# Attention scores of all 24 units in plain float32, two heads in row halves

## The chip, the cores and the metric

The kernel runs on one core of a Trainium2 chip. The metric is the device time of one launch in microseconds (us); lower is better. A core has a matrix engine (PE, with its weight loads shown apart as PEld), a vector engine (DVE), a scalar engine (ACT), GpSimd (POOL) and a queue engine that issues the transfers (SP). Each works through its own instructions in order, and the engines wait for one another through semaphores.

## What is computed

The reference is a gated linear attention (an mLSTM cell) over 4 batches, 8 heads, 768 steps and head size 40, and behind it two dense networks over the 3072 tokens:

```
C = f_stab * C + i_stab * (v k^T);  n = f_stab * n + i_stab * k
y_t = sigmoid(o_t) * (C q_t) / max(|n . q_t|, 1)
x = y as 3072 x 320
x = relu(x @ w_in)^2 @ w_out            (320 -> 2048 -> 320)
x = elu(x @ w2_in) @ w2_out             (320 -> 2048 -> 320)
```

The gates enter through running maxima, so that every exponent stays bounded. All inputs are float32.

## The kernel before, in words

**Tiles and stages.** The sequence is cut into 6 chunks of 128 steps. A unit u is one batch of one chunk (24 units, u = 4 x chunk + batch), and a half n = 2u + e holds the four heads of one parity of that unit. In a unit the chunk is done in parallel: scores K Q^T per head (128 x 128), times a matrix of decays, times V, plus what the state C of the chunks before gives. The first network then takes four units as one tile of 512 tokens. Its 6 tiles times 16 blocks of 128 hidden columns are steps k = 0 to 95; each has 8 matmuls into a bank `h` (mm1, line 501) and 8 into three banks `acc` (mm2, line 546), all 512 columns wide. The second network (lines 582, 612, 626) follows as steps 96 to 191. Weights and activations are held as a rounded high part and a low part (`w`, `xh`/`xl`, `ghi`/`glo`), so that products of fp32r operands reach float32 accuracy.

**How attention and network share the engines.** Attention of tile j + 1 is woven into the steps of tile j. Every step takes one turn t of the attention, four turns to a unit (k = t mod 4). The order in which instructions are issued is the order of the program on every engine. Up to step 19 it is written out by hand: the string ORDER (line 45) is a list of words, each a letter (a task, table at line 788) and a number. So `S16` is the scores of half 16, `p16` the product with its decays, `t7` the transposes of unit 7, `n7` its division, `h7` and `l7` the split of the transposed result, `V8` the values of unit 8 and `Z8` their evacuation, `118`, `216` and `316` are mm1 of step 18 and the two halves of mm2 of step 16, `A` and `F` are the activations and the low part of a step, and `M`, `E` the mask and the exponentials of a half. Behind ORDER the turns do the same by rule, in `attn_pre`, `attn_pe`, `attn_mul`, `attn_post` and `attn_last` (lines 421 to 477).

**The scores.** There are two ways. Halves n < 16 (units 0 to 7, NPLAIN, line 35) use `pair_scores` (line 303). Queries and keys lie as plain float32 in one tile, heads of parity 0 in rows 0 to 39 and heads of parity 1 in rows 64 to 103. Eight matmuls with 40 rows alternate between the halves of the array and write two PSUM banks, `s` and `in` (units 0 to 3 use a bank of `acc` in place of `in`). The profile shows each plain float32 matmul as two records. Halves from 16 up (units 8 to 23) use stacked parts: the host repeats queries and keys three times (120 rows, 480 KB per half); `qk_hi` (line 267, ACT) rounds all to fp32r, `qk_stack` (line 272, DVE, two instructions) turns one third of the rows into the low part, with the factors in `qkm`; then each head is one fp32r matmul over 120 rows (line 320), four to a half, into bank `s` alone. For these units queries are loaded a second time in the row-half layout, as `qp` (line 233), because `values` needs them so.

**The bank `in`.** It is one PSUM bank with several users, each of which waits until the readers of the one before are done: the second half of the plain scores (read by `emit_P`, DVE), the product of queries and state in `values` (line 331, read by `evac`, DVE line 360), the transposes of the normalized result (line 389, read by `x_hi`, ACT line 399, and `x_lo`, DVE lines 406 and 407), and the gates of chunk 1.

**Turns of a unit before.** k = 0: exponentials of the first half, `norm` of unit u - 1, scores and product of the first half. k = 1: exponentials of the second half, `o_tanh`, `wk_mult`, transposes of unit u - 1, scores and product of the second half, `x_hi`, `x_lo`. k = 2: `qk_hi`, `mask` and `qk_stack` for unit u + 1, and then `values` and `evac`. k = 3: loads for unit u + 2.

Of the kernel before, what the change touches and what calls it, by code (L numbers as in the profile page):

```python
# [6 lines left out]
F32 = mybir.dt.float32  # L7
# [14 lines left out]
L = 128  # L22
# [9 lines left out]
KVO = 2 * DM + H * VW  # L32
TT = 4 * L
NTILE = NT // TT
NPLAIN = 16
N0 = 2 * B
TEND = 4 * (NU - 1) + 7
NK = 20
# [9 lines left out]
n1 s3 L0 i2 v5 R3 e6 p6 b2 c2 a2 C1 U1 i3 t1 B8 o2 z4 i2 v6 e7 r0 Q9 p7 M9 k3 z5 n2 v7 o3 E9 h1 z6 z7 b3 l1 n3  # L48
i4 t2 h2 c3 l2 i3 t3 h3 i1 S8 M8 E8 Q10 R4 R5 B11 B10 b4 l3 10 o4 L1 11 a3 A0 p9 H2 L2 R6 12 H3 F0 c4 c5 A1 L3
c6 20 30 M11 21 G2 G3 a4 k4 p8 V4 Q12 13 H4 L4 F1 b5 b6 M10 E10 31 B12 A2 22 a5 H5 K5 Z4 n4 k5 14 L5 t4 R7 c7  # L50
F2 32 b7 a6 H6 R8 g2 R9 Q11 R10 A3 F3 B13 A4 L6 a7 Q16 F4 B14 h4 l4 c8 b8 R11 a8 c9 b9 o5 15 23 A5 H7 L7 a9
c10 Q14 33 F5 K6 24 H8 L8 Q15 16 S10 p10 17 x2 34 E11 25 D2 Q13 H9 L9 p11 A6 b10 A7 a10 F6 35 26 M12 M13 V5
H10 C2 18 36 27 R12 L10 19 R13 E13 y16 o6 F7 37 Z5 c11 b11 a11 B16 n5 c12 U2 A8 110 b12 F8 H11 b13 L11 a12 c13
t5 h5 l5 B15 E12 k6 A9 M14 B17 28 38 K7 k7 H12 Y16 a13 S12 p13 M15 p12 H13 R14 R15 b14 c14 M16 L12 111 F9 A10
F10 29 M17 V6 Z6 n6 B18 E14 112 39 210 310 t6 L13 A11 211 113 a14 H14 c15 b15 a15 H15 h6 l6 F11 E15 A12 S14
p14 q8 A13 K8 p15 F12 311 o7 E17 212 E16 V7 L14 114 F13 Q17 Q18 B19 L15 115 Z7 n7 g3 312 A14 F14 k8 213 M18 q9
t7 h7 l7 S16 p16 y17 y18 313 Y17 Q19 214 Y18 Q20 116 314 A15 117 A16 F16 E18 S17 y19 215 p17 V8 F15 Y19 S18
p18 B20 315 B21 P15 K9 M21 A17 118 216 119 M20 Z8 o8 n8 E20 A18 F17 k9 t8 h8 D3 M19 E19 316 217 K10 F18 S19
q10 A19 317 120 121 p19 x3 l8 F19 y20 Y20 C3 U3 V9 Z9 Q21 y21 Y21 o9 218 A20 318 219 S20 n9 K11 B22 319 p20
Q22 A21 F21 Q23 B23 F20 q11  # L60
"""


def body(tc, qk, qp, kvo, gates, wq, ident_in, qkm_in, out):
    nc = tc.nc
    pe, act, dve, pool_, sp = nc.tensor, nc.scalar, nc.vector, nc.gpsimd, nc.sync
    es = ExitStack()
# [33 lines left out]
    qkm = constp.tile([3 * D, 2], F32, name="qkm")  # L101
    one = constp.tile([64, 1], F32, name="one")
    dve.memset(msk[0:64], 0.0)
    dve.memset(msk[64:128], -1.0)
# [114 lines left out]
            aw_t.pop(c)  # L219


    kvo_t, qp_t, qk_t, mb_t, raw_t, qS, kS, num_t, S_t, PV_t, xt_t, XT_t, X = ({} for _ in range(13))

    def kvo_load(u):

# [7 lines left out]
    def qp_load(u):
        t = a2.tile([128, 4 * L], F32, tag="qp", name="qp")
        sp.dma_start(out=t, in_=qp[u])
        qp_t[u] = t

    def mb_tile(n):
        if n < NPLAIN and n % 2:
# [16 lines left out]

    def qk_load(n):
        u, e = divmod(n, 2)
        if n >= NPLAIN:
            t = raw_t[n] = a2.tile([3 * D, 2, 4 * L], F32, tag="rqk", name="rqk")  # L260
            sp.dma_start(out=t, in_=qk[n])
            return
        if u not in qk_t:
            qk_t[u] = plain[u % B] if u >= B else wp.tile([128, 2 * WC], F32, tag="w", name="rqk")[:, 0:8 * L].rearrange("p (two t) -> p two t", two=2)
        sp.dma_start(out=qk_t[u][64 * e:64 * e + 48], in_=qk[n, 0:48])

    def qk_hi(n):
        st = a2.tile([3 * D, 2, 4 * L], F32R, tag="qks", name="qks")
        act.activation(out=st, in_=raw_t[n], func=AF.Copy)
        qS[n], kS[n] = st[:, 0], st[:, 1]  # L270

    def qk_stack(n):
        t = raw_t.pop(n)
        for i, st in enumerate((qS[n], kS[n])):
            dve.scalar_tensor_tensor(out=st, in0=st.bitcast(F32), scalar=qkm[:, i:i + 1], in1=t[:, i], op0=ALU.mult, op1=ALU.add)

    def keyed(u):
        return u // B < NCH - 1
# [30 lines left out]
                k1, q1 = (t[64 * e:64 * e + D, x, i * L:(i + 1) * L] for x in (1, 0))  # L309
                pe.matmul(S_t[2 * u + e][:, i, :], lhsT=k1, rhs=q1, start=True, stop=True)  # L310

    def scores(n):
        s = bank(n, "s")
        if n < NPLAIN:
            return [lambda: pair_scores(n // 2, (s, bank(n, "in")))]
        s = s.rearrange("p (h t) -> p h t", h=4)
        k_, q_ = kS.pop(n), qS[n]
        S_t[n] = s
        return [
            lambda i=i: pe.matmul(s[:, i, :], lhsT=k_[:, i * L:(i + 1) * L], rhs=q_[:, i * L:(i + 1) * L], start=True, stop=True)  # L320
            for i in range(4)
        ]
# [15 lines left out]
    def values(u):  # L338
        b = u % B
        t = kvo_t[u]  # L340
        q = qk_t.pop(u)[:, 0] if u in qk_t else qp_t.pop(u)
# [441 lines left out]
    def turned(u):  # L783
# [14 lines left out]
    for word in ORDER.split():
# [116 lines left out]
def _layout(inputs):  # L915
# [12 lines left out]
    qp = np.zeros((NU, 128, 4, L), np.float32)  # L928
    for e in range(2):
        qp[:, 64 * e:64 * e + D] = units_t(inputs["q"]).reshape(NU, D, 4, 2, L)[:, :, :, e]  # L930
    qk = np.concatenate([qk] * 3, axis=1)
    qkm = np.zeros((3 * D, 2), np.float32)
    qkm[2 * D:, 0] = -1.0
    qkm[D:2 * D, 1] = -1.0
# [7 lines left out]
    for pre in ("moe_", "moe2_"):  # L942
# [39 lines left out]
```

## Time and profile before

| what | value |
|---|---|
| median of 3 runs | 800.41 us (798.16 to 804.31) |
| the profiled execution | 797.7 us, of which its span is 795.9 us |
| granted TensorE clock | 0.999 of full speed |
| moved by DMA | 88.22 MB |
| query and key loads of units 8 to 23 | 32 of 480 KB, and 16 of 256 KB (`qp`) |
| query and key loads of units 0 to 7 | 16 of 192 KB |

The page of the profile gives busy time by engine, the span in 40 slices, and the groups of instructions that cost most. The busy time of PE says less than it seems to, because the end of a matmul is modelled and matmuls overlap; starts are what the trace has, and the distance from start to start is the cost. In a timeline each row is a run of alike instructions on one engine: start, length, engine, line, operation, output <- inputs, shape and count, and in brackets how long the engine sat idle before and what ended that. A few records of matmuls are missing from the trace, so a count can be lower than the program's.

### The profile page before, as it was taken

How to read it: one execution, taken by the hardware profiler on the slowest of the kernel's cores; microseconds unless marked ns; L12 is line 12 of the kernel's file. 1: busy time of each engine (PE TensorE's matmuls, PEld its weight loads, DVE VectorE, ACT ScalarE, POOL GpSimd, SP SyncE). 2: the span in 40 equal slices, each digit the busy share in tenths (PEclk: the TensorE clock that was granted, in tenths of full speed). 3: DMA queues.
4: the chain of work that ended last, by engine and by line, in shares of the span. 5: the costliest groups of instructions: out<-in, count | busy, mean ns of one | idle time of the engine just before them, and what ended most of it. 6: DMA issues, size and time to landing. Idle time of an engine off the chain costs nothing.

```text
span 795.9 us, 17791 instructions
## 1 busy us (share of the span) xinstructions
PE 786.7 (99%) x7054; PEld 671.7 (84%) x7058; DVE 548.9 (69%) x946; ACT 529.0 (66%) x1028; POOL 143.5 (18%) x209
## 2 busy tenths in 40 slices
PE   8999999999999999999999999999999999999998
PEld 5688788888888888888888889999999999999997
DVE  5898987667666566555348569867677677677765
ACT  5899868677666776777489667565465565555543
POOL 3224201100000001000012123221222122222221
PEclk9999999999999999999999999999999999999999
DMA  8998434955354656551335710300400401300100
GB/s 238 325 284 247 125 101 149 286 152 155 115 162 129 174 132 177 138 164 37 81 112 182 189 41 2 82 34 2 95 20 1 114 2 26 88 2 2 35 1 34
DMA packets 33257, 88.22 MB, mean 111 GB/s; under 512 B 3735, under 2 KB 7319, under 8 KB 33175
## 3 DMA queue, kind: packets, MB, share of 16 engines
q1 hardware_dynamic: 32887, 86.77, 38.7%
q8 instruction: 55, 0.90, 0.5%
q10 hardware_dynamic: 288, 0.33, 0.1%
q14 instruction: 27, 0.22, 0.1%
HBM read 78.35 MB, written 8.73 MB: 109 GB/s over the span
## 4 chain that ended last, share of the span: by engine, by line
PE 87%; DVE 5%; DMA 4%; issue 1%; POOL 1%; SPq 1%; ACT 0%; POOLq 0%; DVEq 0%; ACTq 0%
PE h L582 21%; PE acc L612 20%; PE acc L546 20%; PE h L501 19%; PE pv L331 2%; DMA mb<-negm_dr 2%; PE in L331 2%; PE s L320 2%; DMA raw<-wq 1%; DMA kvo<-kvo 1%; DVE w L150 1%; DVE ct L140 1%; PE in L389 1%; POOL w L144 1%; DVE glo L530 1%
## 5 line engine op out<-in xcount | busy, mean ns | idle before, releaser
L530 DVE TENSOR_TENSOR glo<-r,ghi 128x512 fp32r<-128x512 f32 x192 | 135.6, 707 | 119.2 <-ACT r L516 94.4
L501 PE MATMUL h<-xh,w 128*128 128x512 f32 x576 | 179.8, 394 | 0.0
L612 PE MATMUL acc<-w,ghi 64*128 64x320 f32 x1472 | 142.3, 306 | 0.0
L520 ACT ACTIVATE r<-h 128x512 f32<-128x512 f32 x96 | 56.6, 589 | 116.8 <-PE h L582 116.8
L523 DVE SCALAR_TENSOR_TENSOR ex<-ex,th 128x512 f32<-128x512 f32 x96 | 83.2, 867 | 66.0 <-ACT ex L522 66.0
L501 PEld LDWEIGHTS h<-xh,w 128*128 128x128 f32 x576 | 108.1, 188 | 23.8
L546 PE MATMUL acc<-ghi,w 128*128 128x512 f32 x480 | 127.7, 395 | 0.0
L612 PEld LDWEIGHTS acc<-w,ghi 64*128 64x128 f32 x1472 | 119.4, 184 | 4.1
L525 POOL TENSOR_SCALAR ghi<-r 128x512 fp32r<-128x512 f32 x96 | 74.2, 773 | 264.4 <-DVE r L524 243.7
L546 PEld LDWEIGHTS acc<-ghi,w 128*128 128x128 f32 x480 | 87.5, 188 | 17.5 <-issue 0.4
L612 PE MATMUL acc<-w,glo 64*128 64x320 f32 x736 | 91.4, 306 | 0.0
L515 ACT ACTIVATE ghi<-r 128x512 fp32r<-128x512 f32 x96 | 60.6, 631 | 43.7 <-PE acc L546 42.4
L582 PE MATMUL h<-x,w 64*128 64x512 f32 x720 | 86.7, 388 | 0.0
L514 ACT ACTIVATE r<-h 128x512 f32<-128x512 f32 x96 | 56.6, 589 | 42.5 <-PE h L501 41.2
L546 PE MATMUL acc<-glo,w 128*128 128x512 f32 x288 | 81.8, 392 | 0.0
L582 PEld LDWEIGHTS h<-x,w 64*128 64x128 f32 x720 | 66.4, 184 | 13.5 <-issue 0.7
L501 PE MATMUL h<-xl,w 128*128 128x512 f32 x192 | 74.9, 390 | 0.0
L524 DVE SCALAR_TENSOR_TENSOR r<-h,ex 128x512 f32<-128x512 f32 x96 | 66.4, 692 | 3.3
L612 PEld LDWEIGHTS acc<-w,glo 64*128 64x128 f32 x736 | 63.4, 184 | 0.0
L546 PEld LDWEIGHTS acc<-glo,w 128*128 128x128 f32 x288 | 53.6, 188 | 11.3
L521 ACT ACTIVATE th<-r 128x512 f32<-128x512 f32 x96 | 60.7, 633 | 3.1
L516 ACT ACTIVATE r<-r 128x512 f32<-128x512 f32 x96 | 60.7, 632 | 2.9
(124 smaller groups left out, 1079.3 us busy)
## 6 DMA issues: line engine op xcount, KB each, us to landing
raw<-wq SPq DMA_DIRECT2D x32, 704.0 KB, 6.7
rqk<-qk SPq DMA_DIRECT2D x32, 480.0 KB, 7.9
kvo<-kvo SPq DMA_DIRECT2D x24, 488.0 KB, 5.3
mb<-negm_dr SPq DMA_DIRECT2D x40, 256.0 KB, 5.4
yr<-y_dr SPq DMA_DIRECT2D x12, 768.0 KB, 8.4
y_dr<-y SPq DMA_DIRECT2D x18, 256.0 KB, 3.7
qp<-qp SPq DMA_DIRECT2D x16, 256.0 KB, 6.2
rqk<-qk SPq DMA_DIRECT2D x16, 192.0 KB, 8.8
```

The source lines that it names most:

```text
L501: lambda i=i, a=a, b_=b_: pe.matmul(h[:, 0:n], lhsT=a, rhs=b_, start=(i == 0), stop=(i == len(seq) - 1))
L514: act.activation(out=r, in_=h, func=AF.Relu)
L515: act.activation(out=hi, in_=r, func=AF.Square)
L516: act.activation(out=r, in_=r, func=AF.Square)
L521: act.activation(out=th, in_=r, func=AF.Tanh, scale=0.5)
L523: dve.scalar_tensor_tensor(out=ex, in0=ex, scalar=1.0, in1=th, op0=ALU.add, op1=ALU.mult)
L524: dve.scalar_tensor_tensor(out=r, in0=h, scalar=0.0, in1=ex, op0=ALU.max, op1=ALU.subtract)
L525: pool_.tensor_scalar(out=hi, in0=r, scalar1=1.0, scalar2=1.0, op0=ALU.mult, op1=ALU.mult)
L530: dve.tensor_tensor(out=lo, in0=r, in1=hi.bitcast(F32), op=ALU.subtract)
L546: ops.append(lambda: pe.matmul(o, lhsT=l_, rhs=r_, start=first and st, stop=last and sp_))
L582: pe.matmul(h[i], lhsT=a[r], rhs=b_[r], start=n == 0, stop=n == len(ops) - 1)
L612: pe.matmul(ACC[l, j][i][:, 0:DM], lhsT=a, rhs=b_, start=m == 0 and not again and n == 0, stop=n == 5 and (not again or m + 2 == NF), skip ...
```

## The change

All units use `pair_scores`. `qk_hi`, `qk_stack`, `qp_load`, the tile `qkm` and its load are gone, as are their words in ORDER (`r`, `y`, `Y`, `q`); queries and keys are loaded once, 192 KB per half. The four tiles `plain` serve the units in turn. In the turns the scores of both halves stand at k = 0 and so do both products; the exponentials of the first half move to turn k = 3 of the unit before, those of the second half to k = 0. In ORDER the words `S17` and `S19` go (the scores of a unit are one word now), `p17`, `p19` and `p21` move up behind the first product of their unit, and `Z8`, `M19`, `E19` and `S18` change places. NPLAIN lives on as NEARLY, for the choice of a tile in `mb_tile`.

```diff
 def qk_load(n):
     u, e = divmod(n, 2)
-    if n >= NPLAIN:
-        t = raw_t[n] = a2.tile([3 * D, 2, 4 * L], F32, tag="rqk", name="rqk")
-        sp.dma_start(out=t, in_=qk[n])
-        return
...
-    sp.dma_start(out=qk_t[u][64 * e:64 * e + 48], in_=qk[n, 0:48])
+    sp.dma_start(out=qk_t[u][64 * e:64 * e + 48], in_=qk[n])
-def qk_hi(n):
-    st = a2.tile([3 * D, 2, 4 * L], F32R, tag="qks", name="qks")
-    act.activation(out=st, in_=raw_t[n], func=AF.Copy)
...
-def qk_stack(n):
...
-def scores(n):
-    s = bank(n, "s")
-    if n < NPLAIN:
-        return [lambda: pair_scores(n // 2, (s, bank(n, "in")))]
...
+def scores(u):
+    pair_scores(u, (bank(u, "s"), bank(u, "in")))
 def attn_pre(t):
     if k == 0:
-        units(u, lambda u: emit_E(2 * u))
+        units(u, lambda u: emit_E(2 * u + 1))
...
-        units(u + 1, lambda v: qk_hi(2 * v), lambda v: qk_hi(2 * v + 1), lambda v: mask(2 * v))
-        units(u + 1, lambda v: mask(2 * v + 1), lambda v: qk_stack(2 * v), lambda v: qk_stack(2 * v + 1))
+        units(u + 1, lambda v: mask(2 * v), lambda v: mask(2 * v + 1))
     else:
+        units(u + 1, lambda v: emit_E(2 * v))
-        units(u + 2, lambda v: mb_load(2 * v), lambda v: mb_load(2 * v + 1), qp_load)
...
 def attn_pe(t):
     if k == 0:
-        units(u, lambda u: [f() for f in scores(2 * u)])
+        units(u, scores)
     elif k == 1:
         units(u - 1, lambda w: [f() for f in trans(w)])
-        units(u, lambda u: [f() for f in scores(2 * u + 1)])
 def attn_mul(t):
-    if k < 2:
-        units(u, lambda u: emit_P(2 * u + k))
+    if k == 0:
+        units(u, lambda u: emit_P(2 * u), lambda u: emit_P(2 * u + 1))
```

The end of ORDER, from `V7` on (before, then after):

```
V7 L14 114 F13 Q17 Q18 B19 L15 115 Z7 n7 g3 312 A14 F14 k8 213 M18 q9 t7 h7 l7 S16 p16 y17 y18 313 Y17 Q19 214 Y18 Q20 116 314 A15 117 A16 F16 E18 S17 y19 215 p17 V8 F15 Y19 S18 p18 B20 315 B21 P15 K9 M21 A17 118 216 119 M20 Z8 o8 n8 E20 A18 F17 k9 t8 h8 D3 M19 E19 316 217 K10 F18 S19 q10 A19 317 120 121 p19 x3 l8 F19 y20 Y20 C3 U3 V9 Z9 Q21 y21 Y21 o9 218 A20 318 219 S20 n9 K11 B22 319 p20 Q22 A21 F21 Q23 B23 F20 q11

V7 L14 114 F13 Q17 Q18 B19 L15 115 Z7 n7 g3 312 A14 F14 k8 213 M18 t7 h7 l7 S16 p16 313 Q19 p17 214 Q20 116 314 A15 117 A16 F16 E18 215 V8 F15 B20 315 B21 P15 K9 A17 118 Z8 M19 E19 216 S18 p18 p19 119 M21 M20 o8 n8 E20 A18 F17 k9 t8 h8 D3 316 217 K10 F18 A19 317 120 121 x3 l8 F19 C3 U3 V9 Z9 Q21 o9 E21 218 A20 318 219 S20 n9 K11 B22 319 p20 p21 Q22 A21 F21 Q23 B23 F20
```

## Rows read from the trace of the kernel before

**Rows 1.** The page, part 1: busy us, share of the span, instructions.
```profile
PE 786.7 (99%) x7054; PEld 671.7 (84%) x7058; DVE 548.9 (69%) x946; ACT 529.0 (66%) x1028; POOL 143.5 (18%) x209
```

**Rows 2.** Timeline of PE, three later steps without scores; in the first two, one group of transposes.
```profile
386.37 1.29 PE L546 MATMUL acc<-ghi,w 128*128 128x512 f32 x5
...
393.99 1.29 PE L546 MATMUL acc<-ghi,w 128*128 128x512 f32 x5
...
397.62 1.30 PE L546 MATMUL acc<-ghi,w 128*128 128x512 f32 x5
```

**Rows 3.** Timeline of PE, three steps with both scores of unit 12 and transposes of unit 11.
```profile
166.42 1.31 PE L546 MATMUL acc<-ghi,w 128*128 128x512 f32 x5
...
174.43 0.64 PE L320 MATMUL s<-qks 120*128 120x128 f32 x4
...
178.62 1.29 PE L546 MATMUL acc<-ghi,w 128*128 128x512 f32 x5
```

**Rows 4.** Timeline of PE, plain scores of unit 7 between two groups of the network.
```profile
92.74 0.39 PE L501 MATMUL h<-xh,w 128*128 128x512 f32 x1
...
95.44 0.27 PE L310 MATMUL s<-rqk 40*128 40x128 f32 x1
...
95.56 0.27 PE L310 MATMUL s<-rqk 40*128 40x128 f32 x1
...
95.76 0.97 PE L546 MATMUL acc<-glo,w 128*128 128x512 f32 x3
96.57 1.31 PE L546 MATMUL acc<-ghi,w 128*128 128x512 f32 x5
```

**Rows 5.** Groups by line and form: busy us, mean ns, idle before and its releaser.
```profile
L275 DVE SCALAR_TENSOR_TENSOR qks<-qks,qkm,rqk 120x512 fp32r<-120x512 f32 x64 | 44.0, 746 | 6.6 <-ACT qks L269 6.3
L269 ACT ACTIVATE qks<-rqk 120x1024 fp32r<-120x1024 f32 x32 | 32.3, 1050 | 5.8 <-DMA rqk<-qk 4.6 <-DVE glo L530 1.2
```

**Rows 6.** Timeline of PE, transposes of unit 6.
```profile
88.97 0.84 PE L546 MATMUL acc<-glo,w 128*128 128x512 f32 x3
90.54 0.41 PE L389 MATMUL in<-ident,xt 128*128 128x128 f32 x2 [0.73 <-DVE xt L380]
...
91.51 1.40 PE L546 MATMUL acc<-ghi,w 128*128 128x512 f32 x5
```

**Rows 7.** Timeline of DVE, from the first `qk_stack` to the end of the division of unit 6.
```profile
80.29 1.40 DVE L275 SCALAR_TENSOR_TENSOR qks<-qks,qkm,rqk 120x512 fp32r<-120x512 f32 x2
81.62 0.98 DVE L140 TENSOR_TENSOR ct<-ct,cu 128x704 uint16<-128x704 uint16 x1
...
88.93 0.17 DVE L377 SCALAR_TENSOR_TENSOR den<-num 128x8 f32<-128x8 f32 x1
...
89.90 0.49 DVE L380 SCALAR_TENSOR_TENSOR xt<-kvo,num 128x320 f32<-128x320 f32 x1
```

**Rows 8.** Timeline of PE, transposes of unit 7 and the first stacked scores.
```profile
105.35 0.49 PE L389 MATMUL in<-ident,xt 128*128 128x128 f32 x3
105.59 0.64 PE L320 MATMUL s<-qks 120*128 120x128 f32 x4
```

**Rows 9.** Timeline of DVE, first and last of a stretch without idle time.
```profile
95.86 0.69 DVE L326 TENSOR_TENSOR mb<-s,mb 128x512 f32<-128x512 f32 x1 [0.92 <-PE in L310]
...
107.41 0.34 DVE L407 SCALAR_TENSOR_TENSOR xh<-xh,msk,in 128x128 fp32r<-128x128 f32 x1
```

**Rows 10.** Timeline of PE, transposes of unit 8.
```profile
121.97 0.38 PE L389 MATMUL in<-ident,xt 128*128 128x128 f32 x2
122.69 0.33 PE L389 MATMUL in<-ident,xt 128*128 128x128 f32 x1 [0.34 <-POOL xt L381]
```

**Rows 11.** Timeline of PE, plain scores of unit 4 and the first mm1.
```profile
34.24 0.34 PE L310 MATMUL in<-rqk 40*128 40x128 f32 x1 [0.37 <-DMA rqk<-qk]
...
35.29 0.50 PE L501 MATMUL h<-xh,w 128*128 128x512 f32 x1
```

**Rows 12.** Timeline of DVE, the split that the first mm1 reads.
```profile
34.84 0.34 DVE L407 SCALAR_TENSOR_TENSOR xh<-xh,msk,xt 128x128 fp32r<-128x128 f32 x1
```

More of the change, by code (lines that the diff above doesn't have):

```diff
@@ L34 @@
 NTILE = NT // TT
-NPLAIN = 16
+NEARLY = 16
 N0 = 2 * B
@@ L47 @@
 Q7 R2 o1 n0 s1 i1 t0 h0 Q8 m5 e5 p2 B9 p3 i2 s2 a0 e4 l0 c1 v3 b1 v2 z2 p4 p5 m6 m7 a1 K3 i1 v4 H0 K4 k2 H1 z3
[L48 to L60, printed above, removed]
+n1 s3 L0 i2 v5 R3 e6 p6 b2 c2 a2 C1 U1 i3 t1 B8 o2 z4 i2 v6 e7 Q9 p7 M9 k3 z5 n2 v7 o3 E9 h1 z6 z7 b3 l1 n3 i4
+t2 h2 c3 l2 i3 t3 h3 i1 S8 M8 E8 Q10 R4 R5 B11 B10 b4 l3 10 o4 L1 11 a3 A0 p9 H2 L2 R6 12 H3 F0 c4 c5 A1 L3 c6
@@ new lines @@
+20 30 M11 21 G2 G3 a4 k4 p8 V4 Q12 13 H4 L4 F1 b5 b6 M10 E10 31 B12 A2 22 a5 H5 K5 Z4 n4 k5 14 L5 t4 R7 c7 F2
+32 b7 a6 H6 R8 g2 R9 Q11 R10 A3 F3 B13 A4 L6 a7 Q16 F4 B14 h4 l4 c8 b8 R11 a8 c9 b9 o5 15 23 A5 H7 L7 a9 c10
+Q14 33 F5 K6 24 H8 L8 Q15 16 S10 p10 17 x2 34 E11 25 D2 Q13 H9 L9 p11 A6 b10 A7 a10 F6 35 26 M12 M13 V5 H10 C2
+18 36 27 R12 L10 19 R13 E13 o6 F7 37 Z5 c11 b11 a11 B16 n5 c12 U2 A8 110 b12 F8 H11 b13 L11 a12 c13 t5 h5 l5
+B15 E12 k6 A9 M14 B17 28 38 K7 k7 H12 a13 S12 p13 M15 p12 H13 R14 R15 b14 c14 M16 L12 111 F9 A10 F10 29 M17 V6
@@ new lines @@
+Z6 n6 B18 E14 112 39 210 310 t6 L13 A11 211 113 a14 H14 c15 b15 a15 H15 h6 l6 F11 E15 A12 S14 p14 A13 K8 p15
+F12 311 o7 E17 212 E16 V7 L14 114 F13 Q17 Q18 B19 L15 115 Z7 n7 g3 312 A14 F14 k8 213 M18 t7 h7 l7 S16 p16 313
+Q19 p17 214 Q20 116 314 A15 117 A16 F16 E18 215 V8 F15 B20 315 B21 P15 K9 A17 118 Z8 M19 E19 216 S18 p18 p19
+119 M21 M20 o8 n8 E20 A18 F17 k9 t8 h8 D3 316 217 K10 F18 A19 317 120 121 x3 l8 F19 C3 U3 V9 Z9 Q21 o9 E21 218
+A20 318 219 S20 n9 K11 B22 319 p20 p21 Q22 A21 F21 Q23 B23 F20
@@ L61, with body @@
 """
-def body(tc, qk, qp, kvo, gates, wq, ident_in, qkm_in, out):
+def body(tc, qk, kvo, gates, wq, ident_in, out):
     nc = tc.nc
@@ L100, in body @@
     dve.memset(sel.bitcast(F32), 0.0)
-    qkm = constp.tile([3 * D, 2], F32, name="qkm")
+    constp.tile([128, 2], F32, name="room2")
     one = constp.tile([64, 1], F32, name="one")
@@ L219, in gate_put @@
             aw_t.pop(c)
-    kvo_t, qp_t, qk_t, mb_t, raw_t, qS, kS, num_t, S_t, PV_t, xt_t, XT_t, X = ({} for _ in range(13))
+    kvo_t, qk_t, mb_t, num_t, S_t, PV_t, xt_t, XT_t, X = ({} for _ in range(9))
     def kvo_load(u):
@@ L231, in kvo_load @@
         kvo_t[u] = t
[L233 to L236, printed above, removed]
     def mb_tile(n):
-        if n < NPLAIN and n % 2:
+        if n < NEARLY and n % 2:
             return yp.tile([128, 4, L], F32, tag="y", name="mb")
@@ L258, in qk_load @@
         u, e = divmod(n, 2)
-        if n >= NPLAIN:
-            t = raw_t[n] = a2.tile([3 * D, 2, 4 * L], F32, tag="rqk", name="rqk")
-            sp.dma_start(out=t, in_=qk[n])
-            return
         if u not in qk_t:
             qk_t[u] = plain[u % B] if u >= B else wp.tile([128, 2 * WC], F32, tag="w", name="rqk")[:, 0:8 * L].rearrange("p (two t) -> p two t", two=2)
-        sp.dma_start(out=qk_t[u][64 * e:64 * e + 48], in_=qk[n, 0:48])
-    def qk_hi(n):
-        st = a2.tile([3 * D, 2, 4 * L], F32R, tag="qks", name="qks")
-        act.activation(out=st, in_=raw_t[n], func=AF.Copy)
-        qS[n], kS[n] = st[:, 0], st[:, 1]
-    def qk_stack(n):
-        t = raw_t.pop(n)
-        for i, st in enumerate((qS[n], kS[n])):
-            dve.scalar_tensor_tensor(out=st, in0=st.bitcast(F32), scalar=qkm[:, i:i + 1], in1=t[:, i], op0=ALU.mult, op1=ALU.add)
+        sp.dma_start(out=qk_t[u][64 * e:64 * e + 48], in_=qk[n])
     def keyed(u):
@@ L310, in pair_scores @@
                 pe.matmul(S_t[2 * u + e][:, i, :], lhsT=k1, rhs=q1, start=True, stop=True)
-    def scores(n):
-        s = bank(n, "s")
-        if n < NPLAIN:
-            return [lambda: pair_scores(n // 2, (s, bank(n, "in")))]
[L316 to L322, printed above, removed]
+    def scores(u):
+        pair_scores(u, (bank(u, "s"), bank(u, "in")))
     def emit_P(n):
@@ L340, in values @@
         t = kvo_t[u]
-        q = qk_t.pop(u)[:, 0] if u in qk_t else qp_t.pop(u)
+        q = qk_t.pop(u)[:, 0]
         ps, pi = bank(u, "pv"), bank(u, "in")
@@ L427, in attn_pre @@
         elif k == 1:
-            units(u, lambda u: emit_E(2 * u + 1), o_tanh, wk_mult)
-            if u + 1 == NPLAIN // 2:
-                qk_load(NPLAIN + 1)
+            units(u, o_tanh, wk_mult)
         elif k == 2:
-            units(u + 1, lambda v: qk_hi(2 * v), lambda v: qk_hi(2 * v + 1), lambda v: mask(2 * v))
-            units(u + 1, lambda v: mask(2 * v + 1), lambda v: qk_stack(2 * v), lambda v: qk_stack(2 * v + 1))
-        else:
-            units(u + 2, lambda v: mb_load(2 * v), lambda v: mb_load(2 * v + 1), qp_load)
-            units(u + 2, lambda v: qk_load(2 * v), lambda v: None if v == NPLAIN // 2 else qk_load(2 * v + 1))
+            units(u + 1, lambda v: mask(2 * v), lambda v: mask(2 * v + 1))
+        else:
+            units(u + 1, lambda v: emit_E(2 * v))
+            units(u + 2, lambda v: mb_load(2 * v), lambda v: mb_load(2 * v + 1), lambda v: qk_load(2 * v), lambda v: qk_load(2 * v + 1))
         if k % 2 == 0:
@@ L788, in body @@
     tasks = {
-        "i": idle, "r": lambda _: sp.dma_start(out=qkm, in_=qkm_in),
-        "Q": qk_load, "K": kvo_load, "q": qp_load, "B": mb_load, "R": w_load, "G": gate_load, "D": gate_store,
+        "i": idle,
+        "Q": qk_load, "K": kvo_load, "B": mb_load, "R": w_load, "G": gate_load, "D": gate_store,
         "g": gate, "x": gate_exp, "C": each(gate_cols), "U": gate_put,
@@ L794, in body @@
         "b": w_top, "c": w_low, "a": w_add, "H": w_hi, "L": w_lo,
-        "M": mask, "E": emit_E, "S": each(scores), "V": values, "Z": evac, "y": qk_hi, "Y": qk_stack,
+        "M": mask, "E": emit_E, "S": lambda n: scores(n // 2), "V": values, "Z": evac,
         "1": each(mm1), "A": elem, "F": elem_lo, "2": high_products, "3": low_products, "P": put,
@@ L927, in _layout @@
     qk = qk.transpose(0, 4, 1, 2, 3, 5).reshape(NHU, D, 2, 4 * L)
[L928 to L934, printed above, removed]
+    qk = np.pad(qk, ((0, 0), (0, 8), (0, 0), (0, 0)))
     v = units(inputs["v"])
@@ L956, in _layout @@
     return {
-        "qk": np.ascontiguousarray(qk), "qp": qp.reshape(NU, 128, 4 * L), "kvo": np.ascontiguousarray(kvo), "gates": np.ascontiguousarray(gates),
-        "wq": wq, "ident": np.eye(128, dtype=np.float32), "qkm": qkm,
+        "qk": np.ascontiguousarray(qk), "kvo": np.ascontiguousarray(kvo), "gates": np.ascontiguousarray(gates),
+        "wq": wq, "ident": np.eye(128, dtype=np.float32),
     }
```

## The prediction

> **What bounds the kernel now.** I read the page's busy shares first: PE is busy for 786.7 of the span of 795.9 us, DVE for 548.9 and ACT for 529.0 [rows 1]. Since the busy time of PE is modelled, I went on to its timeline and measured from start to start. Two steps of the first network with one group of transposes in them take 393.99 - 386.37 = 7.62 us, the step behind them 397.62 - 393.99 = 3.63 [rows 2]. That is 16 matmuls of 512 columns at 0.227 us each; the transposes of a unit cost 7.62 - 2 x 3.63 = 0.36. The steps in which unit 12 has its scores are as regular [rows 3]. So from about 125 us on nothing but the length of PE's own list sets the time: what the change takes from ACT, DVE and the queues there is worth nothing, and what it adds to PE is paid in full. Before that, in the order written by hand, PE stands still in a few places, and there the other engines count.
>
> **The change part by part.**
>
> *Scores on PE, 16 units.* Stacked: from 166.42 to 178.62 are 12.20 us for three steps, two groups of stacked scores and one group of transposes [rows 3]. Less 3 x 3.63 and 0.36, that leaves 0.95 us for the eight fp32r matmuls of a unit, their borders included. Plain: mm1 before the scores of unit 7 starts at 92.74 and needs 8 x 0.227, to 94.56. The next network matmul starts at 95.76, 1.20 later, and the three from there take 0.81 where 0.68 is usual, so 0.13 more [rows 4]. A unit thus costs 1.33 us. Inside, two records (one of each row half) start every 0.11 us, and there are eight such pairs, 0.88; the rest is the border to either side. The difference is 0.38 us a unit, and for 16 units **+6.1 us**. Nothing hides it. Its bounds: if the borders cost no more than those of the stacked groups did, 0.88 against 0.95 gives -1.1 us; if the half that waits for bank `in` adds 0.1 in each unit, +7.7. I take 6.1, since the same eight matmuls between the same neighbours are in the trace.
>
> Of this the Trainium skill has a rule, in "FP8 and Floating Point Precision", section "TensorE Precision Notes": true FP32 goes through the array in four passes, while reduced FP32 reads the word cut to fewer bits. It speaks against the change. An estimate from it, with one pass for fp32r, 128 columns a pass at 2.4 GHz and the two halves side by side, is 4 x 0.213 against 8 x 0.053 us, so +0.43 a unit, 6.8 us in all. The rows say two records and 0.22 us for a plain pair, which fits four passes, but borders that take part of the gain from the short stacked matmuls.
>
> *`qk_hi` and `qk_stack` go.* They took 32.3 us of ACT and 44.0 of DVE [rows 5]. Behind 125 us they lay beside PE, worth 0. In the order by hand one place counts: the transposes of unit 6. PE has finished mm2 at 88.97 + 3 x 0.227 = 89.65 and could go on 0.24 later, but does so at 91.51, so it loses 1.6 us to the division of unit 6 on DVE [rows 6]. DVE ran without a break from the first `qk_stack` (80.29) to the end of that division (90.39); `qk_stack` itself took 1.33 of it [rows 7]. Without it the division ends near 89.1 to 89.3, before PE asks. **-1.6 us**; bounds -1.6 and -1.0, if a wait for the values of unit 6 takes back part of the DVE time. I take the first because 1.3 us ahead is enough for all but the GpSimd copy. The scores of unit 7 are late next, and they follow this by 1.1 us or more less in DVE's list.
>
> *Scores of unit 8 (`S16`) now need bank `in`.* In the order they stand right behind `t7`, whose result lies in `in` until `h7` and `l7` have read it. Before, `S16` wrote only `s` and started at 105.59, as soon as the transposes were issued [rows 8]. `l7` ended at 107.41 + 0.34 = 107.75. DVE was without idle time from the product of unit 7 (95.86, the end of idling 0.92 for those scores) to there [rows 9]; none of these instructions goes, for `Y17` and `Y18` stand behind `p16`. So DVE arrives 12 us behind the scores of unit 7 as before, PE after 9.8, and PE waits **+2.2 us**. Queued behind the waiting matmul is everything on PE: mm2 of step 13 and mm1 of step 16 next. Bounds: 0, if DVE should be through earlier by all of it, and 2.5. I take 2.2, since both ends are rows.
>
> *`S18`, `p18`, `p19` before `n8` and `t8`.* Now `Z8` comes before the scores of unit 9 and `n8` behind both products. Between the end of `V8` and `t8` PE has 24 network matmuls and the scores, 24 x 0.227 + 1.3 + 0.1 = 6.9 us. The scores end 4.9 behind `V8`; the two products take 1.3 (0.69 each, overlapping) [rows 9]; the division 89.90 + 0.49 - 88.93 = 1.46 [rows 7]; the copy on GpSimd behind it I estimate at 0.6, so the last transpose starts at 8.3 where 7.1 was possible: a stall of 1.2. Before, the last transpose came 0.72 behind the first, where 0.16 is the pace of a third of 0.24 [rows 8, 10], so a stall of 0.6. **+0.6 us**; bounds -0.6 (no stall) and +1.2.
>
> *Transfers.* 32 loads shrink from 480 to 192 KB; 16 loads of `qp` and the load of `qkm` go, with their issues on SP. PE waits once for such a load, 0.37 us in the scores of unit 4 [rows 11], and the load of `qkm` stood right before that one in SP's list. It still gains nothing: the mm1 behind these scores starts at 35.29, and its last input is split until 34.84 + 0.34 = 35.18 on DVE [rows 12]. 0; bounds -0.4 and 0.
>
> *The turns.* The exponentials of the first half move one turn ahead, those of the second likewise; ACT has lost two `qk_hi` per unit, the masks they need are issued a turn earlier still. Queued behind them on ACT is the activation of that step, whose result PE uses two steps later, some 5.5 us after its own input is ready. 0. Both products now stand at k = 0, and the transposes at k = 1 must wait for the second (bank `in`). Between scores and transposes PE has 16 network matmuls, 3.6 us; DVE needs 1.3 for the products. 0; bounds 0 and, if DVE came 2.8 us late in all 13 units, +6.
>
> **Sum.** 6.1 - 1.6 + 2.2 + 0.6 = +7.3 us on the profiled execution's 797.7, so 805.0. The median of the runs shown is 2.7 above that execution, so I forecast 807.7 for the median: 0.9% slower. A measurement of this kernel can tell about 1%, some 8 us, from no change; the forecast lies just inside.
>
> **The rivals.**
>
> *A. The two waits do not come* (DVE reaches `l7` and `n8` in time). The lighter DVE and SP speak for it; against it, DVE had no idle time in the one case, and in the other the products now precede the division. Then 6.1 - 1.6 - 0.6 = +3.9: 804.3.
>
> *B. The turns wait.* In each of the 13 units behind the order the transposes wait for the second product, because DVE has the division of the unit before in front of it. Slack of 2.3 us speaks against it. With 0.4 us a unit, 5 us more: 812.7.
>
> *C. Not slower: what DVE gives back.* If the stretch by hand, from `Y16` to the last `Y21`, is paced by DVE throughout and PE only looks busy, then 12 `qk_stack` of 0.746 less are 8.95 us there [rows 5], more than the 6.1 and the 0.6 of `t8` together, and with `S16` then in time the sum is -2.3: 798.1. It decides from the point where DVE is the later of the two at every meeting. For it, the unbroken stretches [rows 7, 9]; against it, the idle 0.92 of DVE in front of one of them, and PE's even pace beside it.
>
> *D. The row halves do not overlap in the later units*, so the change doesn't do what it says: 16 records of 0.11 in place of 8 pairs, +0.88 a unit, 14 us more: 821.8. The tiles are built as for units 4 to 7; very little for it.
>
> **How the numbers follow.** Forecast 0.58, A 0.22, B 0.11, C 0.07, D 0.02. Runs scatter by some 3 us to either side. The range is 801 to 813: it takes in A and B and the bounds of the borders, and leaves out C, D and stray medians. Slower by over 1% (above 808.4): about 0.42 of the forecast, B and D, some 0.38 in all. Faster by over 1%: C with luck, 0.03. Within 1%: 0.59.
>
> **What would show it.** Right: plain scores from first to next network matmul near 1.2 us in units 12 to 23; steps of a unit longer by 0.38 in sum; a gap on PE behind `t7` that DVE line 407 ends, near 2 us; a smaller one at `t8`; none at `t6`. Wrong: a PE without gaps at `S16` (A), waits of transposes on line 326 in the turns (B), records of the two halves one behind the other (D), or the end of the first network no later than before (C).

## The result

The changed kernel takes 806.97 us (median of 8 runs, 805.8 to 811.73) against 798.83 us for the kernel before (8 runs): a ratio of 1.0102 with a 95% interval of 1.0073 to 1.0131. It is 8.1 us slower; 7.3 were forecast, 807.7 in all. The sign and the place of each term were right, and the sum was 0.8 too small. That 807.7 came within 0.7 of the median is in part luck: it started from a median of 800.41 (3 runs) for the kernel before, which is 798.83 over 8 runs. The measured 1.02% lies at the bound of 1%, and its interval reaches to both sides of it, so these runs do not tell "within 1%" (0.59) from "slower by over 1%" (0.38); of the 808.4 us that the prediction put at that bound, the median stays short.

The profiled execution of the changed kernel took 809.1 us with a span of 807.3, 11.4 more than that of the kernel before. That is more than the medians differ by, so the two profiles must be read with care: 1.7 us arise before the first mm1 of the network (36.96 in place of 35.29), a point that moves from execution to execution (35.02 in experiment 10), and 1.5 come from a granted clock that fell, as shown below. The page after, part 1:

```profile
PE 794.9 (98%) x7182; PEld 673.3 (83%) x7186; DVE 504.0 (62%) x882; ACT 501.4 (62%) x996; POOL 143.4 (18%) x209
```

Against [rows 1], DVE lost 44.9 us of work and ACT 27.6, 14 MB of transfers are gone (74.59 in place of 88.22), and PE has 8.2 us more. The kernel with the lighter engines is the slower one.

**The regular stretch.** The timeline of PE from the transposes of unit 9 to those of unit 10, one full unit of four turns with its plain scores:

```profile
145.08 0.49 PE L360 MATMUL in<-ident,xt 128*128 128x128 f32 x3
...
163.45 0.49 PE L360 MATMUL in<-ident,xt 128*128 128x128 f32 x3
```

That is 18.37 us. The same two transposes in the kernel before are 18.00 apart:

```profile
138.17 0.49 PE L389 MATMUL in<-ident,xt 128*128 128x128 f32 x3
...
156.17 0.49 PE L389 MATMUL in<-ident,xt 128*128 128x128 f32 x3
```

By the prediction's own pace a unit should now be 4 x 3.63 of network, 0.36 of transposes, 1.33 of scores and the products with the values, which were 18.00 - 14.52 - 0.36 - 0.95 = 2.17 before: 18.38. The difference of 0.37 us a unit comes on PE with no gap beside it.

**The wait at `S16`.** The timeline of PE at the scores of unit 8, in the changed kernel:

```profile
105.77 0.49 PE L360 MATMUL in<-ident,xt 128*128 128x128 f32 x3
106.19 0.49 PE L290 MATMUL s<-rqk 40*128 40x128 f32 x2
108.51 0.34 PE L290 MATMUL in<-rqk 40*128 40x128 f32 x1 [1.84 <-ACT ghi L482]
...
109.85 0.79 PE L513 MATMUL acc<-glo,w 128*128 128x512 f32 x1
111.30 1.94 PE L513 MATMUL acc<-ghi,w 128*128 128x512 f32 x5
```

Its counterpart is [rows 8], where scores followed the transposes at once. Now the matmuls into `s` start, and then PE stands until bank `in` is free. The releaser in brackets is a guess from the profile and misleads here: `ghi` on ACT has nothing to do with the bank. The timeline of DVE shows who it is:

```profile
96.28 0.69 DVE L297 TENSOR_TENSOR mb<-s,mb 128x512 f32<-128x512 f32 x1 [0.90 <-PE in L290]
...
108.07 0.34 DVE L378 SCALAR_TENSOR_TENSOR xh<-xh,msk,in 128x128 fp32r<-128x128 f32 x1
109.59 0.69 DVE L297 TENSOR_TENSOR mb<-s,mb 128x512 f32<-128x512 f32 x1 [1.18 <-PE s L290]
```

DVE worked without a break from 96.28 and read the transposed result for the last time until 108.41; PE went on at 108.51. From 105.77 + 0.24 + 0.1 for the border, that is a wait of 2.4 us. The forecast had 2.2. The rest is on DVE: one scan of the gates (line 191) took 0.73 us in this stretch, 0.47 before; why is not shown.

Behind the gap the matmuls are slow: 1.94 us for five where 1.30 is usual. The windows of one microsecond each say why (stretch and its length; then busy us of PE, PEld, DVE, ACT and POOL with counts; then granted clock, DMA share and GB/s):

```profile
107.00:108.00 1.00, 0.00 (x0) 0.00 (x0) 0.99 (x3) 0.94 (x3) 0.00 (x0) 1.00 0.00 0
108.00:109.00 1.00, 0.49 (x8) 0.52 (x10) 0.41 (x2) 0.59 (x1) 0.00 (x0) 1.00 0.00 0
109.00:110.00 1.00, 1.00 (x12) 0.78 (x8) 0.41 (x1) 0.00 (x0) 0.00 (x0) 0.61 0.00 0
110.00:111.00 1.00, 1.00 (x3) 0.81 (x4) 0.88 (x2) 0.00 (x0) 0.00 (x0) 0.50 0.00 0
111.00:112.00 1.00, 1.00 (x4) 0.81 (x3) 0.00 (x0) 0.00 (x0) 0.00 (x0) 0.50 0.00 0
112.00:113.00 1.00, 1.00 (x4) 0.76 (x4) 0.00 (x0) 0.00 (x0) 0.00 (x0) 0.69 0.00 0
113.00:114.00 1.00, 1.00 (x6) 0.78 (x5) 0.00 (x0) 0.00 (x0) 0.00 (x0) 1.00 0.00 0
```

PE did nothing in 107 to 108 and worked for 0.49 of the microsecond behind it, and for some 3 us from 109.2 it was granted 0.50, the lower of its two levels (1.2 GHz), with matmuls at half pace. That costs 1.5 us, and no step of the forecast had it.

**Transposes of units 6 and 8.** PE, unit 6, beside [rows 6]:

```profile
91.29 0.38 PE L360 MATMUL in<-ident,xt 128*128 128x128 f32 x2
91.84 0.33 PE L360 MATMUL in<-ident,xt 128*128 128x128 f32 x1 [0.17 <-POOL xt L352]
91.93 1.40 PE L513 MATMUL acc<-ghi,w 128*128 128x512 f32 x5
```

From 91.29 to 91.93 are 0.64 us where 0.24 is the pace. The stall of 1.6 us has shrunk to 0.4, which is the GpSimd copy. PE, unit 8, beside [rows 10]:

```profile
126.80 0.84 PE L468 MATMUL h<-xh,w 128*128 128x512 f32 x3
128.68 0.41 PE L360 MATMUL in<-ident,xt 128*128 128x128 f32 x2 [1.03 <-DVE xt L351]
129.29 0.33 PE L360 MATMUL in<-ident,xt 128*128 128x128 f32 x1 [0.20 <-POOL xt L352]
129.37 0.93 PE L513 MATMUL acc<-glo,w 128*128 128x512 f32 x3
```

PE could have gone on to `t8` at 126.80 + 3 x 0.227 = 127.48 and be through at 127.72; the next network matmul starts at 129.37, a stall of 1.65 us, where the forecast had 1.2 and the kernel before 0.56. DVE shows the order that it was foreseen in, products, then division:

```profile
125.80 0.69 DVE L297 TENSOR_TENSOR mb<-s,mb 128x512 f32<-128x512 f32 x1 [3.28 <-ACT mb L281]
126.41 0.68 DVE L297 TENSOR_TENSOR mb<-in,mb 128x512 f32<-128x512 f32 x1
127.01 0.16 DVE L348 SCALAR_TENSOR_TENSOR den<-num 128x8 f32<-128x8 f32 x1
...
128.04 0.49 DVE L351 SCALAR_TENSOR_TENSOR xt<-kvo,num 128x320 f32<-128x320 f32 x1
```

DVE stood idle for 3.28 us in front of these products, with the division of unit 8 (four instructions, 127.01 to 128.53) waiting behind them. What its first three needed was there; the fourth also reads the tanh `o8`, which ACT had done by 125.59 + 0.46 = 126.05, still before the products were through.

### The profile page after: what moved, and what is told of

Same layout as the page of the kernel before. It is cut to its first block, busy times and chain, and to the rows that moved or that the text cites. A ratio compares the mean times of both kernels' runs of the same rounds, so it can differ in the third digit from the quotient of the medians.

```text
span 807.3 us, 17859 instructions
## 1 busy us (share of the span) xinstructions
PE 794.9 (98%) x7182; PEld 673.3 (83%) x7186; DVE 504.0 (62%) x882; ACT 501.4 (62%) x996; POOL 143.4 (18%) x209
## 2 busy tenths in 40 slices
DMA packets 28546, 74.59 MB, mean 92 GB/s; under 512 B 3376, under 2 KB 6960, under 8 KB 28464
## 4 chain that ended last, share of the span: by engine, by line
PE 87%; DVE 5%; DMA 4%; issue 1%; POOL 1%; ACT 1%; SPq 0%; POOLq 0%; DVEq 0%; ACTq 0%
PE h L549 20%; PE acc L579 20%; PE acc L513 20%; PE h L468 19%; PE s L290 2%; PE pv L302 2%; PE in L302 2%; DMA kvo<-kvo 1%; DMA mb<-negm_dr 1%; DVE w L149 1%; POOL w L143 1%; PE dps L693 1%; DVE ct L139 1%; DMA rqk<-qk 1%; PE in L360 1%
## 5 line engine op out<-in xcount | busy, mean ns | idle before, releaser
L513 PE MATMUL acc<-ghi,w 128*128 128x512 f32 x480 | 129.4, 399 | 0.0
```

The costliest lines, as they stand in the source:

```text
L513: ops.append(lambda: pe.matmul(o, lhsT=l_, rhs=r_, start=first and st, stop=last and sp_))
```

## The experiments

**1. The scores of unit 8 later.**

```diff
-l7 S16 p16 313 Q19 p17 214 Q20 116 314
+l7 313 Q19 214 Q20 116 S16 p16 p17 314
```

> The changed kernel with the scores of unit 8 (S16, p16, p17) issued three network groups later, behind mm1 of step 16, so that l7 has read bank in before they start. Theory (the wait for bank in cost 2.4 us there, and the half clock behind it another 1.4 in the profiled execution): no gap on PE behind t7, granted clock 1.00 from 105 to 115 us, and 2.4 to 3.8 us less than the changed kernel's median of 807.0, so 803.2 to 804.6. Rival (the stretch is paced by VectorE, the wait comes back at the next meeting): a gap of like size at V8 or t8, and 806.5 to 807.5.

Measured: 803.69 us (4 runs; ratio to the kernel before 1.0063, 1.0042 to 1.0083), 3.3 us below the changed kernel and in the range of the theory. PE of this kernel:

```profile
105.18 0.49 PE L360 MATMUL in<-ident,xt 128*128 128x128 f32 x3
105.43 0.94 PE L513 MATMUL acc<-glo,w 128*128 128x512 f32 x3
...
109.48 0.37 PE L290 MATMUL s<-rqk 40*128 40x128 f32 x1
109.49 0.37 PE L290 MATMUL in<-rqk 40*128 40x128 f32 x1
```

The network follows the transposes after 0.25 us, both halves of the scores start together, and the mean granted clock of the execution is 1.0. The gap at `t8` is as it was (1.03 and 0.20 of idle time in the brackets there). The wait did not come back: DVE was behind at this one meeting and has slack later (in the changed kernel it idles 6.19 us behind the two products of unit 8).

**2. The division of unit 8 before the scores of unit 9.**

```diff
-315 B21 P15 K9 A17 118 Z8 M19 E19 216 S18 p18 p19 119 M21 M20 o8 n8 E20
+315 B21 o8 P15 K9 A17 118 Z8 M19 n8 E19 216 S18 p18 p19 119 M21 M20 E20
```

> The changed kernel with the division of unit 8 (n8) put before the scores of unit 9 and the masks of unit 10 behind it, o8 earlier still. Theory (t8 waits because n8 stood behind p18 and p19): the 1.65 us gap of PE at the transposes of unit 8 goes, 1.1 to 1.7 us less than the changed kernel, 805.3 to 805.9. Rival (t8 then waits for p19 through bank in, since the exponentials of half 19 come later): a gap of 1 us or more stays at t8, ended by VectorE line 297, and the time is 806.5 to 807.5.

Measured: 806.24 us (4 runs; 1.009, 1.0065 to 1.0116). In the profile the gap at `t8` is gone; its three transposes follow one another without idle time:

```profile
125.93 0.49 PE L360 MATMUL in<-ident,xt 128*128 128x128 f32 x3
```

So the mechanism is as the theory has it, though `o8` moved with `n8` and the two are not told apart. The time is 0.7 us below the changed kernel, less than the 1.1 expected and within the scatter of runs that still have the wait at `S16`; alone, this experiment would not show a gain.

**3. Both**, the edits of experiments 1 and 2 in one kernel.

```diff
-l7 S16 p16 313 Q19 p17 214 Q20 116 314
+l7 313 Q19 214 Q20 116 S16 p16 p17 314
...
-315 B21 P15 K9 A17 118 Z8 M19 E19 216 S18 p18 p19 119 M21 M20 o8 n8 E20
+315 B21 o8 P15 K9 A17 118 Z8 M19 n8 E19 216 S18 p18 p19 119 M21 M20 E20
```

> Both edits of the two runs before in one kernel. Theory (two separate waits on PE in front of work that takes what it takes): the gains add, 3.5 to 5.5 us less than the changed kernel, 801.5 to 803.5, with no gap of PE over 0.3 us from 95 us to the end of the first network. What is left against the kernel before, 3.5 us or so, is then the longer scores less what t6 gains. Rival (the gains overlap): no better than the better of the two.

Measured: 801.87 us (7 runs, 801.55 to 802.44; 1.0038, 1.0025 to 1.0051), 5.1 us below the changed kernel. The gains add: singly they were 3.3 and 0.7 us, and the two gaps of the profile were 2.4 and 1.65. The runs lie close together, 0.9 us from the lowest to the highest, with a mean granted clock of 0.999 or 1.0 in all seven. What is left against the kernel before is 3.5 us, by the interval of the ratio 2.0 to 4.1. The prediction's terms without the two waits give 16 x 0.38 = 6.1, less 1.6 at `t6` and 0.6 at the old `t8`, so 3.9, which lies in it; with the 1.2 that `t6` gave by its stall they make 4.3, just above it. In the one profile, the stretch from the first mm1 to the last transposes is 393.85 - 34.62 = 359.23 us, 4.5 more than before.

**4. The kernel before, with the first `qk_stack` later.**

```diff
-H12 Y16 a13
+H12 a13
...
-310 t6 L13
+310 t6 Y16 L13
```

> The kernel before with one word moved: the first qk_stack (Y16) behind the transposes of unit 6. Theory (this qk_stack made the division of unit 6 late, and the changed kernel gained 1.2 us by its absence): the stall of 1.6 us at those transposes shrinks to 0.4, and the time is 1.2 us below the kernel before, near 797.6. Rival (VectorE is merely shifted, and its 1.3 us come back at the scores of unit 7 or at the next transposes): no change, 798.8, with a new gap of about a microsecond before 107 us.

Measured: 797.0 us (10 runs; 0.9983, 0.9968 to 0.9998), 1.3 us below the kernel before (by the interval 0.2 to 2.6) and the lowest median of this study. PE there:

```profile
90.42 0.84 PE L546 MATMUL acc<-glo,w 128*128 128x512 f32 x3
91.10 0.62 PE L389 MATMUL in<-ident,xt 128*128 128x128 f32 x3
91.48 1.40 PE L546 MATMUL acc<-ghi,w 128*128 128x512 f32 x5
...
94.64 0.48 PE L310 MATMUL s<-rqk 40*128 40x128 f32 x2
95.35 0.34 PE L310 MATMUL in<-rqk 40*128 40x128 f32 x1 [0.23 <-ACT r L516]
...
96.47 0.96 PE L546 MATMUL acc<-glo,w 128*128 128x512 f32 x3
```

The stall of [rows 6] is down to 0.14 us, so that pair of VectorE instructions did make the division late. But about half of the gain goes again at the scores of unit 7, as the rival has it. The bracket there says 0.23 of idle time; from the first score to the network it is 96.47 - 94.64 = 1.83 us, where 1.09 is usual (94.67 to 95.76 in the kernel before). It is the wait for bank `in` once more: DVE, behind the moved `qk_stack`, read the transposes of unit 6 out of it until 94.91 + 0.34 = 95.25. From the first mm1 to the last transposes this execution takes 390.81 - 36.80 = 354.01 us, 0.7 less than the 354.71 of the kernel before.

**5. Scores in the turns twice** (in the kernel of experiment 3).

```diff
-            units(u, scores)
+            units(u, scores, scores)
```

> The kernel with both edits, with the plain scores of the 13 units in the turns (11 to 23) issued twice, the second time over the first. Theory (in the turns the length of PE's list is the time): the second set has no border of its own to the network, so 0.9 to 1.1 us a unit, 12 to 14 us more than the 801.9 of the kernel with both edits: 814 to 816. Rival (PE has slack beside the other engines in the turns): clearly less than 12.

Measured: 818.56 us (one run), 16.7 more, 1.28 us for each of 13 units. All of it is paid, as the theory says, and more than it says: a second set costs nearly as much as the first. Between the sets the starts are 0.32 apart where 0.11 is the pace, so a group of plain scores has a border of its own also to another like it; why is not shown. PE in the last unit:

```profile
388.90 0.27 PE L290 MATMUL in<-rqk 40*128 40x128 f32 x1
389.22 0.37 PE L290 MATMUL s<-rqk 40*128 40x128 f32 x1
...
390.35 1.43 PE L513 MATMUL acc<-ghi,w 128*128 128x512 f32 x5
```

The first set starts at 388.01, so the two take 390.35 - 388.01 = 2.34 us to the network, against 1.09 for one.

**6. The work of ScalarE and VectorE put back** (in the kernel of experiment 3).

```diff
+    def ballast(v):
+        st = a2.tile([48, 2, 4 * L], F32R, tag="bal", name="bal", bufs=1)
+        act.activation(out=st, in_=qk_t[v][0:48], func=AF.Copy)
+        bal.append(st)
+    def ballast_dve(v):
+        st = bal.pop(0)
+        for i in range(2):
+            dve.scalar_tensor_tensor(out=st[:, i], in0=st[:, i].bitcast(F32), scalar=msk[0:48], in1=qk_t[v][0:48, i], op0=ALU.mult, op1=ALU.add)
...
-            units(u + 1, lambda v: mask(2 * v), lambda v: mask(2 * v + 1))
+            units(u + 1, ballast, lambda v: mask(2 * v), ballast_dve, ballast, lambda v: mask(2 * v + 1), ballast_dve)
```

> The kernel with both edits, with the work of qk_hi and qk_stack put back in the turns on scratch data of 48 rows (same lengths per row: 1024 elements on ScalarE, two of 512 on VectorE, for each half of the 13 units 11 to 23), read by nobody. It adds some 27 us to ScalarE and 39 to VectorE. Theory (this work lay beside PE and its removal was worth nothing): 801.9, within 0.8. Rival (the lighter engines gave something back in the turns, and the change would be worse without that): up to 3 us slower, with waits of PE for VectorE in the turns.

Measured: 802.24 us (4 runs; 1.0052, 1.0037 to 1.0067), 0.4 more than experiment 3 and within the 0.8. The instructions put back take as long as those removed (1.05 us on ACT, 0.75 on DVE), and no wait of PE for another engine arises in the turns. The work that the change removes there was worth nothing; the transfers that go with it were not put back, so of them this run says nothing, though PE waited for none there in either kernel.

**7. Row halves one after the other** (in the kernel of experiment 3).

```diff
-        for i in range(4):
-            for e in range(2):
+        for e in range(2):
+            for i in range(4):
```

> The kernel with both edits, with the plain scores of each unit issued half by half, four heads of rows 0 to 39 first and then four of rows 64 to 103, where they alternated. Theory (two records of 0.11 us side by side in the two row halves): eight records more to pay per unit, 0.8 to 0.9 us, in 20 to 24 units, 16 to 21 us more than 801.9: 818 to 823. Rival (the cost of the plain scores is that of issue or of PSUM, not of rows shared): under 5 us more.

Measured: 811.27 us (one run), 9.4 more; neither theory's number. In the turns a unit costs 0.56 more: from `t9` to the last transposes it takes 403.60 - 140.08 = 263.52 us, against 256.26 in experiment 3, for 13 units. The 11 units before them add only 2.1 in all. PE in the last unit:

```profile
381.42 0.82 PE L290 MATMUL s<-rqk 40*128 40x128 f32 x5
381.97 0.37 PE L290 MATMUL in<-rqk 40*128 40x128 f32 x1
382.08 0.27 PE L290 MATMUL s<-rqk 40*128 40x128 f32 x1
...
382.41 0.72 PE L290 MATMUL in<-rqk 40*128 40x128 f32 x5
383.06 1.42 PE L513 MATMUL acc<-ghi,w 128*128 128x512 f32 x5
```

The second half starts 0.55 us after the first, while records of the first still come at 0.11 from each other: for three of the eight places the halves run side by side although the program lists one after the other. The group takes 383.06 - 381.42 = 1.64 us in place of 1.09, and the five places that do not overlap, at 0.11 each, are that difference. So the halves do run side by side, as the theory has it, but the price of losing the alternation is 0.56 of the 0.88 us a unit that rival D of the prediction put on it.

**8. PE kept busy through the wait.**

```diff
+        if u == 8:
+            fill = ident.bitcast(BF16)
+            for _ in range(20):
+                pe.matmul(s[:, 0:256], lhsT=fill[:, 0:128], rhs=fill[:, 0:256], start=True, stop=True)
```

> The changed kernel with 20 matmuls of 256 bf16 columns on the identity, some 2.1 us, issued into bank s just before the scores of unit 8, so that PE works while it would stand at the wait for bank in; the scores overwrite them. Theory (the wait itself is fixed by VectorE and stays; the half clock behind it came from the idle time): scores of unit 8 end no later than in the changed kernel, granted clock 1.00 from 108 to 114 us, time 0 to 1.4 us less than 807.0, as often as the drop comes. Rival (the fill only delays the scores): 1 to 2 us more.

Measured: 806.37 us (4 runs; 1.0104, 1.0087 to 1.0121), 0.6 below the changed kernel. From `t7` to `t8` its profile has 125.81 - 104.49 = 21.32 us, as experiment 10 has with the unfilled wait (21.33): the wait itself stays, and the fill costs nothing. The clock is 1.00 in every window from 104 to 116 us, but so it is in experiment 10, so this run does not show that the fill prevents anything. On the clock it is inconclusive.

**9. The kernel before, with the masks of unit 10 later as well.**

```diff
-K9 M21 A17 118 216 119 M20 Z8 o8 n8 E20
+K9 A17 118 216 119 Z8 o8 n8 M21 M20 E20
```

> The kernel before with Y16 behind the transposes of unit 6 and, besides, the masks of halves 20 and 21 (M21, M20) behind the division of unit 8, so that the GpSimd copy which the transposes of unit 8 wait for does not stand behind masks that wait for a transfer. Theory (the 0.56 us at t8 before was that copy): no gap of PE over 0.3 us at t6 and t8, 0.3 to 0.6 us below the 797.0 of the kernel with Y16 alone, 796.4 to 796.7. Rival (the exponentials of half 20 come late in return, or the difference is lost in scatter): 796.8 to 797.5.

Measured: 798.33 us (12 runs; 0.9997, 0.9986 to 1.0009), above the ranges of both. No gain shows, though the interval overlaps that of experiment 4, so the times alone do not put it behind that one. The trace shows the rival's cause. The gaps at `t6` and `t8` are both gone, and a new one stands behind them; PE, then ACT, of this kernel:

```profile
128.71 0.50 PE L501 MATMUL h<-xh,w 128*128 128x512 f32 x1 [0.97 <-ACT r L514]
```
```profile
123.54 1.28 ACT L301 ACTIVATE mb<-mb,cols 128x128 f32<-128x128 f32 x4 [2.44 <-POOL mb L293]
```

ACT waited 2.44 us for the masks, and the activations of the network stand behind the exponentials in its list. From `t7` to `t9` this execution takes 139.31 - 105.78 = 33.53 us, that of experiment 4 138.90 - 106.06 = 32.84. The mask that had held up a copy now holds up the network.

**10. The changed kernel again**, with no edit.

> The changed kernel as it is, a second time, to see what of its profile is the program's and what the execution's. Theory (the wait for bank in is fixed by VectorE's list, the half clock behind it comes in some executions only): the gap behind t7 again 2.2 to 2.5 us, the one at t8 again 1.6 to 1.7; first mm1 of the network anywhere from 34.6 to 37.1 us; median 805.5 to 807.5, and the runs with a mean granted clock of 0.999 or more at the lower end. Rival (the half clock is part of it each time): granted clock 0.5 for some 3 us behind the scores of unit 8 in the profile again.

Measured: 807.04 us (4 runs; 1.0115, 1.009 to 1.014). PE of this execution:

```profile
35.02 0.50 PE L468 MATMUL h<-xh,w 128*128 128x512 f32 x1
...
103.72 0.49 PE L360 MATMUL in<-ident,xt 128*128 128x128 f32 x3
...
106.47 0.34 PE L290 MATMUL in<-rqk 40*128 40x128 f32 x1 [1.85 <-ACT ghi L482]
...
125.05 0.41 PE L360 MATMUL in<-ident,xt 128*128 128x128 f32 x2 [1.03 <-DVE xt L351]
...
141.45 0.49 PE L360 MATMUL in<-ident,xt 128*128 128x128 f32 x3
...
397.71 0.49 PE L360 MATMUL in<-ident,xt 128*128 128x128 f32 x3
```

The same two gaps to a hundredth, and a granted clock of 1.00 behind the first: from the transposes of unit 7 to those of unit 8 it took 21.33 us, against 22.91 in the first profile, so the half clock was worth 1.58 there and is a matter of the execution. First mm1 at 35.02, near the 35.29 of the kernel before, so this is the profile to account with.

## Why the prediction was right, and where its terms were off

The last transposes on PE of the kernel before:

```profile
390.00 0.49 PE L389 MATMUL in<-ident,xt 128*128 128x128 f32 x3
```

Counted from the first mm1 [rows 11], they come after 390.00 - 35.29 = 354.71 us and those of experiment 10 after 397.71 - 35.02 = 362.69. That is +7.98 us, close to the 8.1 between the medians, and behind it the two kernels are alike. Term by term:

- **Scores, forecast +6.1 (16 x 0.38).** From `t9` to the last transposes, 13 units, the stretch grew from 390.00 - 138.17 = 251.83 to 397.71 - 141.45 = 256.26 us. The kernel before had one group more in it (0.48, the second scores of unit 10), so a unit costs (4.43 + 0.48) / 13 = 0.378 more, 6.05 us in all. Right to a tenth. The borders make it: eight pairs of records are 0.88 us, and 0.45 of the 1.33 lie at the two ends. The estimate that the prediction worked out from "FP8 and Floating Point Precision" of the Trainium skill (section "TensorE Precision Notes") was 0.43 a unit, a little above the 0.378 of the trace.
- **`t6`, forecast -1.6.** Measured -1.2 by the stall (1.62 to 0.40). The step that failed is the one that took the first of two bounds "because 1.3 us ahead is enough for all but the GpSimd copy": the copy was the part that was still late. Experiment 4 confirms the cause, since moving that `qk_stack` alone takes the stall to 0.14 us.
- **`S16` and bank `in`, forecast +2.2.** Measured 2.4, in both profiles, and taken away by experiment 1. What the step lacked is what a gap may bring behind it: half clock, 1.5 us in one of two executions.
- **`t8`, forecast +0.6.** Measured +1.1 (1.65 against 0.56). The order of causes was right. The term was mis-sized by small pieces: the products began 0.2 later behind the scores than I counted, the division and its copy took 1.5 and 0.8 with their waits in place of 1.46 and 0.6.
- **Transfers and the turns, forecast 0.** Right: no gap of PE in the turns of either profile, and experiment 6 puts ScalarE's and VectorE's work of the turns back for 0.4 us.

The three terms of the part written by hand all missed in the same direction, by 0.4, 0.2 and 0.5 us too kind to the change; their mechanisms were right and their sizes off. The measured terms add up to 8.35, where the trace has 7.98; the 0.4 between them is not assigned.

Rival A (the waits do not come) fell with the two gaps, B (the turns wait) with the even units, C (what DVE gives back) with the 0.90 us that DVE still idles before its long stretch and with a sum of +8 in place of -2, and D with the records starting in pairs.

Still open is how often the clock falls, and whether the wait at `S16` brings it. Of the changed kernel's 12 timed runs three have a mean granted clock of 0.999 or 1.0, and these took 805.4, 805.8 and 806.9 us; the lowest clock, 0.991, belongs to the longest, 811.7. All four runs of experiment 2, which keeps that wait, are below 0.999, and only one of the eleven of experiments 1 and 3, which do not have it; but so are 6 of the 16 runs of the kernel before that were taken with them, and it has no wait of that length. Where in those runs it fell is not recorded.

## What to carry to other kernels

Where one engine's list is the time, a change is worth what it does to that list, borders included, and 72 us less on the others can be worth nothing. When a change lets an operation write one more shared bank, look up in the issue order who last reads that bank and how far that engine is behind at that very point; moving the operation by a few places may win back the whole wait. And when a wait in such an order is removed, look at what now stands in front of what, since moving the masks only made the network wait in place of the copy, and moving the first `qk_stack` gave back half of its gain at the next use of bank `in`.

## What the runs showed that I had not expected

- A gap of 2.4 us on PE was followed in one execution by some 3 us at the lower clock level (0.50), worth 1.5 us, and in another execution of the same program by none. The kernel without these gaps had a clock of 0.999 or more in all seven runs of experiment 3 and all four of experiment 6, with a scatter of 0.9 and 0.4 us.
- Row halves that are listed one after the other overlap by themselves for part of the way: 0.56 us lost in a unit, where 0.88 would be the price of no overlap.
- A second group of plain scores right behind the first pays a border of its own, 0.32 us between two starts in place of 0.11.
- One scan of the gates on VectorE took 0.73 us in the changed kernel's profiles, 0.47 at the same place in the kernel before. In the changed kernel two masks ran on GpSimd beside it (104.74 to 106.01 in the first profile), in the kernel before one that had ended; whether that is the cause is not shown.
